# Sparse attention followed by a mixture of depths: half a mask, one count of ranks and one slot compare move between engines

## The chip, the core and the metric

The kernel runs on one core of one Trainium2 chip. The metric is the device time of one execution in microseconds. The median of three runs before the change is 803.54 us. Engines are named as in the profile: PE (TensorE, matmuls; PEld is its weight load), DVE (VectorE), ACT (ScalarE), POOL (GpSimd), SP (SyncE, which here only issues DMAs). Each engine works through its own instructions in order; semaphores order engines among each other.

## The reference

Attention keeps, for each query, only the 32 largest of its 576 scores. Its output is the input of a mixture of depths: the 128 tokens of each batch with the highest gate go through a two-layer network, the others are passed on as they are.

```python
B, H, S, D = 8, 8, 576, 64          # q, k, v: (8, 8, 576, 64) f32
scores = q @ k.T / sqrt(D)
kth = 32nd largest score of each row
attn = softmax(where(scores >= kth, scores, -1e9))
x = (attn @ v) as (B, S, H * D)     # (8, 576, 512)

gate = x @ w_gate                   # (8, 576)
for b in range(B):
    top = the 128 tokens with the largest gate[b]
    h = maximum(x[b, top] @ w1, 0)  # (128, 1024)
    y = h @ w2                      # (128, 512)
    out[b] = x[b]
    out[b, top] = x[b, top] + sigmoid(gate[b, top]) * y
```

## The kernel before

**Units and steps.** The 576 query rows of a batch are cut into five tiles: four of 128 rows, and one of 64 (t = J = 4). A unit is one tile and two heads (four heads for the last tile), so a batch has 4 * 4 + 2 = 18 units and the kernel N = 144. The main loop runs `for n in range(-1, N)`, and step n does something for several units at once, so that the engines overlap: the scores of unit n + 1 on TensorE and their copy `sc` on ScalarE, the bound search of unit n on VectorE, the comparison with the bound of unit n - 1 on ScalarE and GpSimd, the exact 32nd value of unit n - 2 on VectorE, the masks of unit n - 3, and the transposition, exponential and value matmul of unit n - 4. The text calls n modulo 18 the position of a step in its batch; position 0 of batch b is n = 18 b.

**The search on VectorE.** `find_bound` takes the eight largest of each of seven stretches of 82 or 83 scores (14 instructions `cand<-sc` for the two halves of a unit), then reduces these (`best`, `bound`) to the 24th largest of the candidates. ScalarE forms the sign of each score against that bound (`sides`, with the sum in `seen`, lines 561 to 568; `sign` is called once early in a step and once after the score copy). GpSimd multiplies scores and signs (`y`, line 1115) and adds a short filling (`fill`). VectorE takes the eight largest of `y` (`next`); the last of these is the 32nd score.

**The mask.** `mask` (line 585) writes 0 for scores that stay, and something positive for others, in `less`. The first half of a unit goes to ScalarE (Relu with a bias, line 594), the second to GpSimd (`tensor_scalar`, is_lt). In the steps of `scatter_steps` (line 1041: n = 54, 72, 90, 108, 126 and 137) GpSimd has a scatter of rows to issue, and the second half goes to VectorE instead: the pair of engines is `(act, None)`, and None stands for `compare`, an is_lt that also sums. It is put off to the middle of the step's bound search by `vector_late`. TensorE then turns the scores and adds the mask (`turn`, line 633), ScalarE takes the exponential (`pT`).

**The mixture.** When all tiles of a batch have been divided and their gates formed (`dot`, line 979), `mixture` (line 761) runs as a generator, piece by piece, in steps of the next two batches given by `mix_at`. For batches 0 to 6, in this order:

- position 5: `split` on GpSimd (the gates in three bf16 parts); two small DMAs write the gates to DRAM, a third reads them back to every partition as `gate_row`, 128x576.
- positions 7, 9, 10, 13, 14, one for each tile t: `choose` counts on VectorE how many gates are larger than each of the tile's own (`junk<-gate_row,gate`, sum in `ranks`); then a comparison of the rank with the slot numbers 0 to 127 gives `pick`, a 0/1 matrix. For t = 0 that comparison is on VectorE as well, for others on GpSimd (`choose_slot` through `pool_late`). What is put off runs in the step after, so the first tile's is at position 8. Batch 6 uses the closer list of line 1029; its first two tiles are both put off to n = 133.
- position 16: `multiply_places` multiplies `pick` with `parts` into a few free columns of PSUM, which gives each slot its token and gate; then the rows are fetched, multiplied with w1 and w2 at positions 1 to 17 of the batch after, and scattered back with addition (`add_rows`) at position 0 of the one after that.

**What is put off, and where it runs.** `late` is emptied by `flush` on ScalarE's and others' part of the step, before the score copy; `vector_late` between the two halves of the bound search; `pool_late` after the bound search and before GpSimd's products `y`.

```python
for b in rest:
    next(mixtures[b], None)
```

**The end.** After the loop the last units are finished without overlap of further ones, the last batch's mixture is done with its own code (lines 1350 to 1569), and a check is made: several reductions give `sure`, 1 for each partition if all shortcuts were exact; the sum of all ranks must also be that of 0 to 575 for each batch. If not, `tc.If(is_unsure > 0)` runs `general`, which does all eight batches over again in a slower, exact way.

Of the kernel before, what the change touches and what calls it, by code (L numbers as in the profile page):

```python
# [10 lines left out]
AF = mybir.ActivationFunctionType  # L11
ALU = mybir.AluOpType
FP32 = mybir.dt.float32
BF16 = mybir.dt.bfloat16
# [5 lines left out]
CAP = 128  # L20
# [28 lines left out]
def kernel(  # L49
# [11 lines left out]
    nc = tc.nc  # L61
    P = nc.NUM_PARTITIONS
    B, H, S, D = q.shape
# [3 lines left out]
    NT = J + 1  # L67
# [3 lines left out]
    DE = D + 1  # L71
    NDC = HD // P
    NFC = F // P
    scale = 1.0 / float(D) ** 0.5 / SMALLER
# [3 lines left out]
    const = ctx.enter_context(tc.tile_pool(name="const", bufs=1))  # L78
# [40 lines left out]
    for i in range(2):  # L119
        gate = const.tile([P, NT], FP32, name=f"gate{i}")  # L120
        nc.gpsimd.memset(gate, 0.0)
        parts = const.tile([P, NT, 2, 3], BF16, name=f"parts{i}")
        nc.gpsimd.memset(parts, 0.0)
        nc.vector.tensor_copy(out=parts[:, :, 0, 0:2], in_=parts_i)
        gates_of.append((gate, parts))
    slot_i = const.tile([P, CAP], I32, name="slot_i")
    nc.gpsimd.iota(slot_i, pattern=[[1, CAP]], base=0, channel_multiplier=0)
# [25 lines left out]

    ranks = const.tile([P, B, NT], FP32, name="ranks")
    nc.gpsimd.memset(ranks, 0.0)

    others = const.tile([P, NT], FP32, name="others")
    nc.gpsimd.memset(others, 0.0)
# [43 lines left out]

    late, vector_late, pool_late = [], [], []
# [180 lines left out]
    def bank(pool, name, **how):  # L384
        return pool.tile([P, 512], FP32, name=name, **how)
# [199 lines left out]
    def mask(sc, next8, on=None):  # L585

        less = wkpool.tile([P, 2, S], BF16, name="less")  # L590
        for i, engine in enumerate(on or (act, pool)):
            kth = next8[:, i, 7:8]
            if engine is act:
                act.activation(less[:, i, :], sc[:, i, :], AF.Relu, bias=kth, scale=-1.0)
            else:

                def is_less(engine=engine, i=i, kth=kth):
                    if engine is None:
                        compare(less[:, i, :], sc[:, i, :], kth, ALU.is_lt)
                        return  # L600
                    engine.tensor_scalar(
                        out=less[:, i, :],
                        in0=sc[:, i, :],
                        scalar1=kth,
                        scalar2=None,
                        op0=ALU.is_lt,
                    )

                if engine:
                    is_less()  # L610
                else:
                    vector_late.insert(0, is_less)
        return less

    def turn_some(tr, z, less):
# [142 lines left out]
            rank[0:n, t : t + 1], rank[0:n, t : t + 1], tok[0:n, 1:2], ALU.add  # L758
        )

    def mixture(row0, pg, rank, exact=False):

# [28 lines left out]


        pick = modpool.tile([P, NT, CAP], BF16, name="pick")
        for t in range(NT):
            yield
            n = R if t == J else P

            def choose(t=t, n=n):  # L800
                junk = modpool.tile([P, S], FP32, name="junk", tag="scratch")
                dve.tensor_scalar(
                    out=junk[0:n, :],
                    in0=gate_row[0:n, :],
                    scalar1=gate[0:n, t : t + 1],
                    scalar2=None,
                    op0=ALU.is_gt,
                    op1=ALU.add,
                    accum_out=rank[0:n, t : t + 1],
                )  # L810
                if exact:
                    break_ties(t, gate, gate_row, rank)

                if t == 0:
                    compare(pick[:, t, :], slot, rank[:, t : t + 1], ALU.is_equal)
                else:
                    pool_late.append(lambda: choose_slot(t, n))

            def choose_slot(t, n):
                pool.tensor_scalar(  # L820
                    out=pick[0:n, t, :],
                    in0=slot[0:n, :],
                    scalar1=rank[0:n, t : t + 1],
                    scalar2=None,
                    op0=ALU.is_equal,
                )

            vector_late.append(choose)

# [2 lines left out]
            ps = ps_misc.tile([P, 512], FP32, name="place_ps", tag="misc")  # L832
        else:
            ps = values_bank[0]
        ps = ps[:, 2 * DE : 2 * DE + 6]


        done = B if exact else int(row0) // S + 1
        row_i = modpool.tile([P, 1], I32, name="row_i", bufs=2)
        g = modpool.tile([P, 1], FP32, name="g", bufs=2)  # L840
        multiply_places(ps, pick, pg)
        found = stats.tile([P, 6], FP32, name="found", bufs=2)
        place = stats.tile([P, 2], FP32, name="place", bufs=2)
        kept.append(lambda ps=ps: act.copy(out=found, in_=ps))

# [62 lines left out]
    def multiply_places(ps, pick, pg):  # L908

        for t in range(NT):  # L910
            n = R if t == J else P
            pe.matmul(
                ps,
                pick[0:n, t, :],
                pg[1][0:n, t, :, :].rearrange("p a e -> p (a e)"),
                start=(t == 0),
                stop=(t == J),
            )

    def split(gate, parts):  # L920

        rest = modpool.tile([P, NT], FP32, name="rest")
        pool.tensor_copy(out=parts[:, :, 1, 0], in_=gate)
        pool.tensor_tensor(rest, gate, parts[:, :, 1, 0], ALU.subtract)
        pool.tensor_copy(out=parts[:, :, 1, 1], in_=rest)
        pool.tensor_tensor(rest, rest, parts[:, :, 1, 1], ALU.subtract)
        pool.tensor_copy(out=parts[:, :, 1, 2], in_=rest)

    def add_parts(place, found):
        dve.tensor_reduce(  # L930
            out=place,
            in_=found.rearrange("p (a e) -> p a e", e=3),
            axis=mybir.AxisListType.X,
            op=ALU.add,
        )
# [201 lines left out]
    def mask_of(n, on=None):  # L1137
        b, i = divmod(n, per_batch)
        masks[n] = mask(scs[n], next8s[b][:, i, :, :], on)
        if i == per_batch - 1 and b < B - 1:  # L1140
            keep_least(b, bounds.pop(b)[:, :, :, 7], next8s.pop(b)[:, :, :, 7])

    for n in range(-1, N):
# [60 lines left out]
        if is_unit(n - 4):  # L1204
            turn_rest()()
        if is_unit(n - 3):
            mask_of(n - 3, (act, None) if n in scatter_steps else None)
        flush()
        if is_unit(n + 1) and n + 1 >= NHP:
            b, i = divmod(n, per_batch)  # L1210
# [55 lines left out]
        if gating is not None:  # L1266
            b, t = gating
            if t == J:
                store(out[b], of_batch[b][0])
                mixtures[b] = mixture(float(b * S), of_batch[b][1], ranks[:, b, :])  # L1270
        for b in rest:
            next(mixtures[b], None)
        b, i = divmod(n, per_batch)
# [153 lines left out]
    for t in (J - 1, J):  # L1427
# [6 lines left out]
            op0=ALU.subtract,  # L1434
            op1=ALU.is_equal,
        )
    ps = bank(ps_end, "av3")[:, 0:6]
    place = stats.tile([P, 2], FP32, name="place", bufs=2)
    row_i = modpool.tile([P, 1], I32, name="row_i", bufs=2)
    g = modpool.tile([P, 1], FP32, name="g", bufs=2)  # L1440
# [2 lines left out]
    keep_rows(place, row_i, float((B - 1) * S), float(B * S - 1))  # L1443
    xe = modpool.tile([P, HD], FP32, name="xe")
    fetch_rows(xe, out, row_i)
    dve.tensor_scalar_max(out=g, in0=place[:, 1:2], scalar1=-88.0)
    act.activation(g, g, AF.Exp, scale=-1.0)
    for _ in between:
# [42 lines left out]
    for what, op, than, limit in (  # L1491
        (bounded, ALU.min, ALU.is_gt, LEAST),
        (least, ALU.min, ALU.is_gt, LEAST),
        (low, ALU.min, ALU.is_gt, 0.5),
        (seen, ALU.max, ALU.is_lt, float(MIDDLE)),
        (seen, ALU.min, ALU.is_gt, float(MIDDLE - 16)),
        (sums.rearrange("p t h -> p (t h)"), ALU.min, ALU.is_gt, FEWEST),
        (sums.rearrange("p t h -> p (t h)"), ALU.max, ALU.is_lt, MOST),
    ):
        far = stats.tile([P, 1], FP32, name="far", bufs=2)  # L1500
        dve.tensor_reduce(out=far, in_=what, axis=mybir.AxisListType.X, op=op)
        dve.scalar_tensor_tensor(
            out=sure, in0=far, scalar=limit, in1=sure, op0=than, op1=ALU.mult
        )

    far = stats.tile([P, 1], FP32, name="far", bufs=2)
    dve.tensor_reduce(out=far, in_=ranks, axis=mybir.AxisListType.XY, op=ALU.add)
    dve.tensor_tensor(sure, sure, far, ALU.add)
    far = stats.tile([P, 1], FP32, name="far", bufs=2)
    dve.tensor_reduce(out=far, in_=others, axis=mybir.AxisListType.X, op=ALU.add)  # L1510
    dve.tensor_tensor(sure, sure, far, ALU.add)
    ones = stats.tile([P, 1], FP32, name="ones", bufs=1)
    dve.memset(ones, 1.0)
    unsure = const.tile([1, 1], I32, name="unsure")
# [2 lines left out]
    for f0 in range(0, NFC, 2):  # L1517
# [20 lines left out]
        out=unsure,  # L1538
        in0=ps[0:1, 0:1],
        scalar1=-1.0,  # L1540
        scalar2=float(P + B * (S * (S - 1) // 2)),
        op0=ALU.mult,
        op1=ALU.add,
    )
# [133 lines left out]
```

## Time and profile before

| | us |
|---|---|
| median of 3 runs | 803.54 |
| runs | 805.48, 803.54, 802.9 |
| profiled execution, its own time | 802.83 |
| span of its instructions in the profile | 800.5 |
| VectorE busy in the span | 771.6 |
| ScalarE, TensorE, GpSimd busy | 728.4, 728.1, 706.4 |
| granted TensorE clock, mean | 0.997 |

The 2.3 us between the profiled execution and its span lie outside the instructions. Busy time is the union of an engine's recorded instructions. A recorded instruction on VectorE, ScalarE or GpSimd overlaps its successor a little (the 288 `next` instructions have a mean of 751 ns, while two of them in a row start 0.67 us apart), so what one costs is read from the starts. Nearly all of the kernel's calls pass through one helper, so they carry its line, L45, and are told apart by the tiles they write and read.

### The profile page before, as it was taken

How to read it: one execution, taken by the hardware profiler on the slowest of the kernel's cores; microseconds unless marked ns; L12 is line 12 of the kernel's file. 1: busy time of each engine (PE TensorE's matmuls, PEld its weight loads, DVE VectorE, ACT ScalarE, POOL GpSimd, SP SyncE). 2: the span in 40 equal slices, each digit the busy share in tenths (PEclk: the TensorE clock that was granted, in tenths of full speed). 3: DMA queues.
4: the chain of work that ended last, by engine and by line, in shares of the span. 5: the costliest groups of instructions: out<-in, count | busy, mean ns of one | idle time of the engine just before them, and what ended most of it. 6: DMA issues, size and time to landing. Idle time of an engine off the chain costs nothing. (4 is left out here: it accounts for less than half of the span.)

```text
span 800.5 us, 33285 instructions
## 1 busy us (share of the span) xinstructions
PE 728.1 (91%) x12535; PEld 550.2 (69%) x12535; DVE 771.6 (96%) x4655; ACT 728.4 (91%) x1577; POOL 706.4 (88%) x722
## 2 busy tenths in 40 slices
PE   8888888788999999999999989999899999999887
PEld 6766666656876668766786667866687667767756
DVE  7999999999999999999999999999999999999962
ACT  6999999999999999999999999999999999989830
POOL 4899999899999999999999999999999999999921
PEclk9999999999999999999999999999999999999999
DMA  8941114121241132221251221502234102101021
GB/s 170 293 95 43 42 62 103 29 54 29 70 107 42 29 94 63 64 55 41 69 109 29 56 41 62 113 20 54 42 90 89 29 8 75 24 6 25 3 74 31
DMA packets 121752, 50.70 MB, mean 63 GB/s; under 512 B 116016, under 2 KB 116016, under 8 KB 120560
## 3 DMA queue, kind: packets, MB, share of 16 engines
q1 hardware_dynamic: 118368, 43.94, 22.2%
q0 software_dynamic: 1744, 4.20, 2.8%
q8 instruction: 101, 1.65, 0.9%
q10 hardware_dynamic: 1472, 0.36, 0.2%
q14 instruction: 67, 0.55, 0.2%
HBM read 36.93 MB, written 11.55 MB: 61 GB/s over the span
## 5 line engine op out<-in xcount | busy, mean ns | idle before, releaser
L45 POOL TENSOR_TENSOR y<-sc,sides 128x576 f32<-128x576 f32 x288 | 366.9, 1304 | 17.7 <-ACT sides L45 16.6
L45 DVE MAX8 cand<-sc 128x8 f32<-128x82 f32 (+1 forms) x2016 | 314.4, 228 | 3.0 <-ACT sc L45 3.0
L45 POOL TENSOR_SCALAR less<-sc,next 128x576 bf16<-128x576 f32 x135 | 232.5, 1722 | 38.4 <-DVE next L45 34.2
L45 ACT ACTIVATE sides<-sc,bound 128x576 bf16<-128x576 f32 x288 | 229.6, 797 | 17.0 <-DVE bound L45 13.1
L45 PEld LDWEIGHTS av<-v,pT 128*64 128x64 f32 x4608 | 146.9, 138 | 91.4 <-ACT last L45 83.8
L45 DVE MAX8 next<-y 128x8 f32<-128x584 f32 x288 | 204.4, 751 | 0.0
L45 PE MATMUL av<-v,pT 128*64 128x65 f32 x4608 | 166.9, 225 | 38.9 <-ACT last L45 38.4
L45 PEld LDWEIGHTS <-less 64*128 64x128 bf16 (+1 forms) x2448 | 157.6, 129 | 29.3 <-POOL less L45 24.6
L45 PE MATMUL ps<-kT,qT 64*128 64x288 f32 (+1 forms) x1248 | 170.1, 422 | 0.3 <-ACT sc L45 0.3
L45 PE MATMUL ptr<-out_of_reach,less 64*128 64x64 bf16 x2272 | 151.0, 190 | 17.3 <-POOL less L45 16.6
L45 PE MATMUL ptr<-ident,sc 64*128 64x64 f32 x2272 | 166.3, 252 | 0.0
L45 ACT ACTIVATE pT<-ptr 128x1024 f32<-128x1024 f32 x142 | 147.7, 1040 | 14.5 <-PE ptr L45 12.7
L45 ACT COPY sc<-ps 128x1152 f32<-128x1152 f32 x140 | 159.6, 1140 | 0.0
L45 PEld LDWEIGHTS ptr<-ident,sc 64*128 64x128 f32 x2272 | 138.6, 137 | 23.8 <-issue 21.2
L45 ACT ACTIVATE less<-sc,next 128x576 bf16<-128x576 f32 x141 | 110.5, 784 | 0.0
L45 PEld LDWEIGHTS ps<-kT,qT 64*128 64x128 f32 (+1 forms) x1248 | 92.8, 176 | 17.6 <-ACT sc L45 0.4
L45 DVE MATCH_REPLACE8 cand<-best,cand 128x21 f32<-128x21 f32 (+1 forms) x576 | 98.8, 179 | 0.0
L45 DVE MAX8 best<-cand 128x8 f32<-128x21 f32 (+1 forms) x576 | 90.4, 189 | 0.0
L45 ACT ACTIVATION_READ_ACCUMULATOR sides<-sc,bound 128x1 f32 x288 | 62.0, 215 | 0.0
L45 PE MATMUL h_ps<-xeT,w 128*128 128x128 f32 x464 | 61.9, 278 | 0.0
L45 PEld LDWEIGHTS av<-ident,sc 128*128 128x128 f32 x144 | 20.0, 139 | 54.8 <-issue 44.9
L45 PE MATMUL av<-vpair,last 128*64 128x130 f32 x576 | 56.9, 276 | 0.0
(165 smaller groups left out, 925.2 us busy)
## 6 DMA issues: line engine op xcount, KB each, us to landing
v<-in_v_dram SPq DMA_DIRECT2D x64, 128.0 KB, 3.7
out_dram<-x SPq DMA_DIRECT2D x8, 1024.0 KB, 4.1
rows<-in_k_dram SPq DMA_DIRECT2D x56, 128.0 KB, 2.8
rows<-in_q_dram SPq DMA_DIRECT2D x56, 128.0 KB, 2.9
w<-in_moe_w_dram SPq DMA_DIRECT2D x2, 2048.0 KB, 10.3
gate_row<-row_dram SPq DMA_DIRECT2D x7, 288.0 KB, 4.6
last<-in_q_dram SPq DMA_DIRECT2D x8, 128.0 KB, 3.6
vpair<-in_v_dram SPq DMA_DIRECT2D x16, 64.0 KB, 4.8
```

The lines of the kernel that those rows point to most:

```text
L45: return lambda *a, **kw: self._tc.keep_in_program_order(fn(*a, **kw))
```

## The change

Four things are changed.

1. In `scatter_steps` both halves of the mask are on ScalarE, `(act, act)`; `mask` no longer has a VectorE form.
2. In the mixtures of batches 0 to 6 the first tile's count is made on ScalarE: the sum of Sign(gate - gate_row) over the 576 gates. With r gates larger than one's own that sum is 575 - 2 r. It is put off through `late`; the signs themselves are written over `pick` and not used.
3. The first tile's comparison with the slots goes to GpSimd, which compares the sum with `slot_signs` = 575 - 2 * slot.
4. `parts` has a seventh column of ones, so `multiply_places` also counts how many tokens each slot received. These counts are kept in `places` for all batches, and the check at the end asks that each be one, in place of the sum of the ranks.

```diff
@@ constants
-        parts = const.tile([P, NT, 2, 3], BF16, name=f"parts{i}")
+        parts = const.tile([P, NT, 7], BF16, name=f"parts{i}")
         nc.gpsimd.memset(parts, 0.0)
-        nc.vector.tensor_copy(out=parts[:, :, 0, 0:2], in_=parts_i)
+        nc.gpsimd.memset(parts[:, :, 6:7], 1.0)
+        nc.vector.tensor_copy(out=parts[:, :, 0:2], in_=parts_i)
...
+    signs = const.tile([P, B - 1], FP32, name="signs")
+    places = const.tile([P, B, 7], FP32, name="places")
+    nc.gpsimd.memset(places, 1.0)
+    slot_signs = const.tile([P, CAP], FP32, name="slot_signs")
+    nc.vector.tensor_scalar(
+        out=slot_signs, in0=slot, scalar1=-2.0, scalar2=float(S - 1),
+        op0=ALU.mult, op1=ALU.add,
+    )
@@ mixture
         for t in range(NT):
             yield
             n = R if t == J else P
+
+            def weigh_gates():
+                act.activation(
+                    pick.rearrange("p t c -> p (t c)")[:, 0:S],
+                    gate_row,
+                    AF.Sign,
+                    bias=gate[:, 0:1],
+                    scale=-1.0,
+                    accum_out=sign_sum,
+                )
+                pool_late.append(lambda: choose_slot(0, P, slot_signs, sign_sum))
+
+            if t == 0 and not exact:
+                late.append(weigh_gates)
+                continue
...
-                if t == 0:
-                    compare(pick[:, t, :], slot, rank[:, t : t + 1], ALU.is_equal)
-                else:
-                    pool_late.append(lambda: choose_slot(t, n))
+                pool_late.append(lambda: choose_slot(t, n))
...
-        ps = ps[:, 2 * DE : 2 * DE + 6]
+        ps = ps[:, 2 * DE : 2 * DE + 7]
...
-        found = stats.tile([P, 6], FP32, name="found", bufs=2)
+        found = places[:, 0 if exact else done - 1, :]
@@ main loop
-            mask_of(n - 3, (act, None) if n in scatter_steps else None)
+            mask_of(n - 3, (act, act) if n in scatter_steps else None)
@@ end
     fetch_rows(xe, out, row_i)
+    act.copy(out=places[:, B - 1, 6:7], in_=ps[:, 6:7])
...
+        (places[:, :, 6], ALU.min, ALU.is_gt, 0.5),
+        (places[:, :, 6], ALU.max, ALU.is_lt, 1.5),
...
-    dve.tensor_reduce(out=far, in_=ranks, axis=mybir.AxisListType.XY, op=ALU.add)
-    dve.tensor_tensor(sure, sure, far, ALU.add)
-    far = stats.tile([P, 1], FP32, name="far", bufs=2)
-    dve.tensor_reduce(out=far, in_=others, axis=mybir.AxisListType.X, op=ALU.add)
-    dve.tensor_tensor(sure, sure, far, ALU.add)
```

More of the change, by code (lines that the diff above doesn't have):

```diff
@@ L155 @@
     nc.gpsimd.memset(ranks, 0.0)
+    signs = const.tile([P, B - 1], FP32, name="signs")
[3 more added lines that the diff above has]
+    nc.vector.tensor_scalar(
+        out=slot_signs,
+        in0=slot,
+        scalar1=-2.0,
+        scalar2=float(S - 1),
+        op0=ALU.mult,
+        op1=ALU.add,
+    )
     others = const.tile([P, NT], FP32, name="others")
@@ L595, in mask @@
             else:
[L597 to L610, printed above, removed]
-                else:
-                    vector_late.insert(0, is_less)
+                engine.tensor_scalar(
+                    out=less[:, i, :],
+                    in0=sc[:, i, :],
+                    scalar1=kth,
+                    scalar2=None,
+                    op0=ALU.is_lt,
+                )
         return less
@@ L759, in break_ties, with mixture @@
         )
-    def mixture(row0, pg, rank, exact=False):
+    def mixture(row0, pg, rank, exact=False, sign_sum=None):
         gate = pg[0]
@@ L795, in mixture, with choose_slot @@
         pick = modpool.tile([P, NT, CAP], BF16, name="pick")
+        rank_of = rank
+        def choose_slot(t, n, slot=slot, rank=None):
+            if rank is None:
+                rank = rank_of[:, t : t + 1]
+            pool.tensor_scalar(
+                out=pick[0:n, t, :],
+                in0=slot[0:n, :],
+                scalar1=rank[0:n, :],
+                scalar2=None,
+                op0=ALU.is_equal,
+            )
         for t in range(NT):
@@ L798, in mixture @@
             n = R if t == J else P
+            def weigh_gates():
[6 more added lines that the diff above has]
+                    accum_out=sign_sum,
+                )
+                pool_late.append(lambda: choose_slot(0, P, slot_signs, sign_sum))
+            if t == 0 and not exact:
+                late.append(weigh_gates)
+                continue
             def choose(t=t, n=n):
@@ L812, in choose @@
                     break_ties(t, gate, gate_row, rank)
-                if t == 0:
-                    compare(pick[:, t, :], slot, rank[:, t : t + 1], ALU.is_equal)
-                else:
-                    pool_late.append(lambda: choose_slot(t, n))
[L819 to L826, printed above, removed]
+                pool_late.append(lambda: choose_slot(t, n))
             vector_late.append(choose)
@@ L914, in multiply_places @@
                 pick[0:n, t, :],
-                pg[1][0:n, t, :, :].rearrange("p a e -> p (a e)"),
+                pg[1][0:n, t, :],
                 start=(t == 0),
@@ L922, in split @@
         rest = modpool.tile([P, NT], FP32, name="rest")
[L923 to L927, printed above, removed]
+        pool.tensor_copy(out=parts[:, :, 3], in_=gate)
+        pool.tensor_tensor(rest, gate, parts[:, :, 3], ALU.subtract)
+        pool.tensor_copy(out=parts[:, :, 4], in_=rest)
+        pool.tensor_tensor(rest, rest, parts[:, :, 4], ALU.subtract)
+        pool.tensor_copy(out=parts[:, :, 5], in_=rest)
     def add_parts(place, found):
@@ L931, in add_parts @@
             out=place,
-            in_=found.rearrange("p (a e) -> p a e", e=3),
+            in_=found[:, 0:6].rearrange("p (a e) -> p a e", e=3),
             axis=mybir.AxisListType.X,
@@ L1269 @@
                 store(out[b], of_batch[b][0])
-                mixtures[b] = mixture(float(b * S), of_batch[b][1], ranks[:, b, :])
+                mixtures[b] = mixture(
+                    float(b * S),
+                    of_batch[b][1],
+                    ranks[:, b, :],
+                    sign_sum=signs[:, b : b + 1],
+                )
         for b in rest:
@@ L1436 @@
         )
-    ps = bank(ps_end, "av3")[:, 0:6]
+    ps = bank(ps_end, "av3")[:, 0:7]
     place = stats.tile([P, 2], FP32, name="place", bufs=2)
@@ L1504 @@
         )
-    far = stats.tile([P, 1], FP32, name="far", bufs=2)
-    dve.tensor_reduce(out=far, in_=ranks, axis=mybir.AxisListType.XY, op=ALU.add)
-    dve.tensor_tensor(sure, sure, far, ALU.add)
-    far = stats.tile([P, 1], FP32, name="far", bufs=2)
-    dve.tensor_reduce(out=far, in_=others, axis=mybir.AxisListType.X, op=ALU.add)
-    dve.tensor_tensor(sure, sure, far, ALU.add)
     ones = stats.tile([P, 1], FP32, name="ones", bufs=1)
@@ L1540 @@
         scalar1=-1.0,
-        scalar2=float(P + B * (S * (S - 1) // 2)),
+        scalar2=float(P),
         op0=ALU.mult,
```

## The prediction, made before the changed kernel was run

> **What bounds the kernel now.** I read the page's busy shares first, then the busy time of one batch's 18 steps, then the waits, then the instructions of two steps one by one.
>
> ```profile
> PE 728.1 (91%) x12535; PEld 550.2 (69%) x12535; DVE 771.6 (96%) x4655; ACT 728.4 (91%) x1577; POOL 706.4 (88%) x722
> ```
>
> Four engines are nearly full, so shares alone decide nothing. Batch 5's steps (its scores; n = 90 to 107), cut at position 9, in the columns PE, PEld, DVE, ACT, POOL:
>
> ```profile
> 471.75:518.31 46.56, 44.23 (x790) 36.00 (x786) 46.45 (x287) 45.60 (x101) 43.97 (x45) 1.00 0.34 82
> 518.31:566.33 48.02, 45.10 (x767) 30.91 (x767) 47.99 (x291) 45.31 (x98) 44.23 (x44) 1.00 0.17 41
> ```
>
> VectorE is idle for 0.14 of 94.58 us. The others have 3.7 us (ScalarE), 6.4 (GpSimd) and 5.3 (TensorE) to spare, mostly in the second half. The waits of that batch (engine waiting, for whom; us in total, times, longest):
>
> ```profile
> POOL less L45 <- DVE next L45: 5.5, 10, 1.0
> ...
> ACT sides L45 <- DVE bound L45: 2.2, 5, 0.6
> PE ptr L45 <- POOL less L45: 2.2, 7, 0.6
> ```
>
> GpSimd and ScalarE wait for VectorE; no line has VectorE waiting. So in the loop the time is the sum of VectorE's instructions. From the timeline (start, us), position 0 (n = 90, a scatter's step), and below it position 8 (n = 98):
>
> ```profile
> 472.77 0.79 DVE L45 TENSOR_SCALAR_CACHE_REDUCE less<-sc,next 128x576 bf16<-128x576 f32 x1
> 473.49 0.08 DVE L45 DVE_READ_ACCUMULATOR less<-sc,next 128x1 f32 x1
> 473.49 1.11 DVE L45 MAX8 cand<-sc 128x8 f32<-128x82 f32 x7
> ```
>
> ```profile
> 512.38 1.10 DVE L45 MAX8 cand<-sc 128x8 f32<-128x82 f32 x7
> 513.40 0.18 DVE L45 RECIPROCAL rden<-sums 128x8 f32<-128x8 f32 x1
> 513.50 0.76 DVE L45 TENSOR_SCALAR_CACHE_REDUCE junk<-gate_row,gate 128x576 f32<-128x576 f32 x1
> 514.19 0.08 DVE L45 DVE_READ_ACCUMULATOR junk<-gate_row,gate 128x1 f32 x1
> 514.31 0.34 DVE L45 TENSOR_SCALAR_CACHE_REDUCE pick<-slot,ranks 128x128 bf16<-128x128 f32 x1
> 514.58 0.08 DVE L45 DVE_READ_ACCUMULATOR pick<-slot,ranks 128x1 f32 x1
> 514.58 1.11 DVE L45 MAX8 cand<-sc 128x8 f32<-128x82 f32 x7
> ```
>
> An instruction starts before the last one's recorded end, so its price is the distance between starts, not its duration. The mask costs 473.49 - 472.77 = 0.72 us; the count with the first slot's compare costs 514.58 - 513.50 = 1.08, of which 0.12 is the compare's wait for the rank.
>
> **The change part by part.**
>
> *Removed from VectorE.* The mask goes from six steps (n = 54, 72, 90, 108, 126, 137): 6 x 0.72 = 4.3 us. Count and compare go from seven mixtures: six at 1.08, and the seventh (n = 133, where the next tile's count follows) 1.11 from 697.81 to 698.92: 7.6 us. Together 11.9. Whole steps say the same: position 0 without a mask (n = 36) lasts 4.74 against 5.47, position 8 5.93 against 4.80 for a step that also has a reciprocal (n = 102), so 6 x 0.73 + 7 x 1.13 = 12.3. I take 11.9.
>
> *Added to ScalarE.* A mask half and a Sign with a sum, priced by ScalarE's own rows:
>
> ```profile
> 475.93 0.78 ACT L45 ACTIVATE sides<-sc,bound 128x576 bf16<-128x576 f32 x1 [0.65 <-DVE bound L45]
> 476.62 0.19 ACT L45 ACTIVATION_READ_ACCUMULATOR sides<-sc,bound 128x1 f32 x1
> 476.71 0.26 ACT L45 ACTIVATE last<-av 128x128 f32<-128x128 f32 x1
> 476.87 0.76 ACT L45 ACTIVATE less<-sc,next 128x576 bf16<-128x576 f32 x1
> 477.53 0.63 ACT L45 COPY kT<-ps 128x256 f32<-128x256 f32 x2
> ```
>
> The mask is 477.53 - 476.87 = 0.66. The Sign with its accumulator read is 0.78 here, and 0.77 over the loop. A batch gains 1.43 us of ScalarE, all in positions 0 to 8. Both kinds already run there under the trace's single table load, so no load is added. TensorE's wait for VectorE's mask at a scatter (0.2 in this batch) goes; GpSimd's mask is then the last that it waits for, as elsewhere. Queued behind them are the copies of K and Q, the score copy of the next step, and the second Sign, for which GpSimd's products wait.
>
> Is there room? Positions 0 to 8: VectorE falls to 46.56 - 1.80 = 44.76, ScalarE rises to 45.60 + 1.43 = 47.03. It falls back by at most 2.3 us. Positions 9 to 17: 48.02 against 45.31, so 2.7 us are made up before the next batch. VectorE does not feel this while its inputs are early, and they are. At n = 98 it starts on scores at 512.38 and on products at 516.98. These were ready at 509.63 and 513.18:
>
> ```profile
> 508.38 1.25 ACT L45 COPY sc<-ps 128x1152 f32<-128x1152 f32 x1
> ```
>
> ```profile
> 512.97 0.21 POOL L45 TENSOR_TENSOR y<-steps,seen 128x16 f32<-128x16 f32 x1
> ```
>
> That is 2.75 us ahead with ScalarE already about 0.95 late there (its first Sign of a step starts 0.95 after the bound that it needs), 3.8 when it is on time. A lateness of 2.3 leaves 1.5. So the cost is nothing; what hides it is VectorE's own stock of finished scores.
>
> The skill's page "ScalarE: Activation LUTs" (Rules for kernel authors) speaks against this move: simple elementwise work belongs on VectorE, up to about 3 times as fast in bf16. By that rule a 576-wide pass would cost VectorE some 0.24 us (0.72 / 3, an estimate from page and row), 13 passes 3.1, and with 7 x 0.39 for compares and bubbles the gain would be 5.9 us, the time 797.6. The rows say 0.72: with an f32 source and a sum, VectorE takes as long as ScalarE. I follow the rows.
>
> *Added to GpSimd.* Seven compares of 128x128. Three in a row run from 706.35 to 708.08, 0.577 each: 4.0 us. Each stands at position 8 behind the division and ahead of the two products. It waits for the Sign, which ScalarE issues before the second Sign that the products wait for anyway, so it adds work and no new wait. The products of n = 97 end 0.58 later than at 518.54, at 519.1. VectorE reads them 1.08 earlier than about 522.3 (518.31, plus 3.4 as in step 98 without its 1.08 and the reciprocal, plus 0.6 for a dot), at 521.2: 2.1 us are left. The next mask half follows later, and TensorE's turn waits for it (0.6 once per batch now, perhaps 1.5 then); that again makes ScalarE late, not VectorE. GpSimd's positions 0 to 8 hold 43.97 + 0.58 = 44.6 us of work in 44.76.
>
> *Data.* The Sign needs gate_row. In batch 5 its load is issued at 501.8 and takes 4.6 us, while the Sign would start at about 513.7; for the seventh mixture it is issued at 690.4 and needed at about 697.9, still 2.9 us to spare. No transfer is moved.
>
> *Start and end.* One more VectorE instruction (slot_signs) at 3.8 us: the nearest row, 128x128, took 0.23; VectorE then idles until 4.85. Three more memsets on GpSimd, whose last one ended at 4.18, 0.03 to 0.1 each: 0 to 0.2 us, and TensorE's first transpose at 4.37 stood behind its own warm-up; I take 0. At the end four small reductions and products are replaced by four (0.6 us either way), done 2.5 us before TensorE needs their result at 788.11. The extra ScalarE copy of one column (about 0.2) fits into the 0.85 that ScalarE idles before Exp at 776.23. Seven columns instead of six in a 0.17 us matmul: nothing.
>
> Sum: -11.9 us. The profiled execution took 802.83 (span 800.5), so 790.9; on the median of 803.54, 791.6.
>
> **The rivals.**
>
> *VectorE begins to wait.* GpSimd's later mask holds up TensorE, that ScalarE, that the scores, and the 2.1 us melt at positions 8 to 10. For it: GpSimd fills 44.6 of 44.76 us, and TensorE, ScalarE and GpSimd wait for each other in a ring. Against it: every observed lateness is made up within three steps. If half of six times 1.08 and a third of six times 0.72 is given back (6 x 0.54 + 6 x 0.24 = 4.7): 796.3.
>
> *ScalarE becomes the bound.* Its batch is 90.9 + 1.43 = 92.3 against VectorE's 92.8. If its waits of about 1.5 us (pT, and Signs) cannot be removed, a batch takes 93.8, only 0.8 less than now: 6 x 0.8, about 799. Against it: most of these waits exist because it is ahead.
>
> *Slower: the end's check fails.* Exactness decides. At its own place a gate gives Sign(0), which must add exactly 0; if it added 1 or -1, the sum would have the wrong parity for every slot, slots of the first tile stay empty, and the new check (0.5 < filled < 1.5) sends all eight batches through the general path. That path needs 14 passes of 576 per unit on VectorE; two of 584 take 1.33 (470.42 to 471.75), so 144 x 14 x 0.67 = 1,350 us at least: over 2,100. One unfilled slot is enough. Nothing in this trace shows a Sign of exact zero, so the case stays open. It is also the case in which the change does not do what it says.
>
> **How the numbers follow.** VectorE stays the bound: 0.77, giving 791.6 (790.3 to 793). It waits in part: 0.13, 793 to 798. ScalarE the bound: 0.06, 798 to 802. Check fails: 0.04. A measurement here tells about 0.3% (2.4 us) from no change, so half of the ScalarE case counts as the same: faster 0.93, same 0.03, slower 0.04. Downwards the range takes 12.3 for 11.9, the lowest of the three runs and some of the tail's waits: 789.5. Upwards it takes most of the second case: 796.
>
> **What would show it.** Right: steps at positions 0 and 8 of about 4.75 and 4.85 us; VectorE still 99.8% busy between 100 and 740; ScalarE's and GpSimd's busy time up by 9.4 and 4.0; scores still 1 us or more ahead of VectorE. Wrong: idle time of VectorE before cand (waiting for sc) or next (waiting for y), above all at positions 8 to 10; the general path's instructions after the last scatter.

## The result, and the profile after

| | before | changed |
|---|---|---|
| median, us (runs) | 804.27 (4) | 793.24 (4) |
| range, us | 802.90 to 805.48 | 792.51 to 794.72 |
| profiled execution / its span, us | 802.83 / 800.5 | 794.72 / 792.5 |
| VectorE, ScalarE, GpSimd busy, us | 771.6, 728.4, 706.4 | 763.2, 732.9, 713.5 |

The ratio is 0.9866, with a 95% interval of 0.9842 to 0.9889. In a later set of runs the changed kernel took 794.18 (793.98 to 795.72) beside 802.93 (14 runs, 802.38 to 805.28): 0.9895, 0.988 to 0.991. So the change brings 8.7 to 11.0 us; the profiled pair (a long run of the changed kernel, a short one of the kernel before) differs by 8.0 of span.

The page's busy line of the changed kernel:

```profile
PE 726.9 (92%) x12535; PEld 551.2 (70%) x12535; DVE 763.2 (96%) x4616; ACT 732.9 (92%) x1598; POOL 713.5 (90%) x732
```

Batch 5 again, from the start of n = 90 to that of n = 99 and on to n = 108 (columns PE, PEld, DVE, ACT, POOL):

```profile
467.56:512.26 44.70, 42.77 (x778) 34.77 (x774) 44.63 (x281) 44.53 (x100) 42.85 (x45) 1.00 0.35 86
512.26:560.67 48.41, 46.22 (x781) 32.14 (x779) 48.38 (x290) 46.98 (x102) 46.42 (x45) 1.00 0.17 41
```

The first half lasts 44.70 in place of 46.56: the 1.86 that mask and count were worth. But the second half lasts 48.41 in place of 48.02, though nothing was added to VectorE there. VectorE is still idle for 0.10 of 93.11 us. The waits of this batch that answer to those shown of before have shrunk, since GpSimd and ScalarE have less slack behind VectorE (one other has grown: GpSimd's products wait for ScalarE's Sign, 0.2 us before and 1.2 now):

```profile
POOL less L45 <- DVE next L45: 1.8, 4, 0.5
...
PE ptr L45 <- POOL less L45: 1.0, 3, 0.4
...
ACT sides L45 <- DVE bound L45: 0.4, 1, 0.4
```

VectorE's timeline, first at position 0 (14 stretches without a mask between them), then at position 8 (no count, no compare, only the reciprocal):

```profile
467.56 2.12 DVE L45 MAX8 cand<-sc 128x8 f32<-128x82 f32 x14
```

```profile
507.46 1.10 DVE L45 MAX8 cand<-sc 128x8 f32<-128x82 f32 x7
508.48 0.18 DVE L45 RECIPROCAL rden<-sums 128x8 f32<-128x8 f32 x1
508.58 1.07 DVE L45 MAX8 cand<-sc 128x8 f32<-128x82 f32 x7
```

What went to ScalarE at position 8 stands back to back there (start, us):

```profile
508.51 0.77 ACT L45 ACTIVATE less<-sc,next 128x576 bf16<-128x576 f32 x1
509.18 0.76 ACT L45 ACTIVATE pick<-gate_row,gate 128x576 bf16<-128x576 f32 x1
509.84 0.19 ACT L45 ACTIVATION_READ_ACCUMULATOR pick<-gate_row,gate 128x1 f32 x1
509.93 0.36 ACT L45 COPY kT<-ps 128x256 f32<-128x256 f32 x1
```

The Sign and its accumulator cost 509.93 - 509.18 = 0.75, forecast 0.77.

**Where the second half's 0.4 us lies.** At position 9 the only VectorE instruction that changed is the gate's dot, which was neither moved nor edited. VectorE and GpSimd around it, first before the change:

```profile
519.62 0.67 DVE L45 CUSTOM_DVE_ANT_0 prod<-x,wg 128x512 f32<-128x512 f32 x1
520.22 0.08 DVE L45 DVE_READ_ACCUMULATOR2_ANT gate<- 128x1 f32 x1
```

```profile
515.85 2.51 POOL L45 TENSOR_TENSOR y<-sc,sides 128x576 f32<-128x576 f32 x2
518.33 0.21 POOL L45 TENSOR_TENSOR y<-steps,seen 128x16 f32<-128x16 f32 x1
518.59 1.72 POOL L45 TENSOR_SCALAR less<-sc,next 128x576 bf16<-128x576 f32 x1
```

and after it:

```profile
513.57 1.07 DVE L45 CUSTOM_DVE_ANT_0 prod<-x,wg 128x512 f32<-128x512 f32 x1
514.58 0.08 DVE L45 DVE_READ_ACCUMULATOR2_ANT gate<- 128x1 f32 x1
```

```profile
510.95 0.61 POOL L45 TENSOR_SCALAR pick<-slot_signs,signs 128x128 bf16<-128x128 f32 x1
511.53 2.52 POOL L45 TENSOR_TENSOR y<-sc,sides 128x576 f32<-128x576 f32 x2
514.00 0.72 POOL L45 TENSOR_TENSOR y<-steps,seen 128x16 f32<-128x16 f32 x1
```

Before, the dot started 1.26 us after the end of GpSimd's products (518.36) and cost 520.22 - 519.62 = 0.60. Now it starts 0.48 us ahead of their end (511.53 + 2.52 = 514.05) and costs 514.58 - 513.57 = 1.01. Its end lies 0.58 behind the start of GpSimd's next instruction (514.58 - 514.00), so it needs about its usual 0.60 once the products are over; in turn that next instruction, GpSimd's small filling, which took 0.21, takes 0.72 and ends as the dot ends. All of this is recorded as busy time, on both engines. No wait row shows it, and that is why VectorE looks as full as before. The view of the tile `prod` (duration of its 40 dots in ns: least, median, most) before and after:

```profile
L45 DVE CUSTOM_DVE_ANT_0 prod<-x,wg x40: 668/680/1596, 50.3 to 771.0; 128x512 f32<-128x512 f32 x32, 64x512 f32<-64x512 f32 x8
```

```profile
L45 DVE CUSTOM_DVE_ANT_0 prod<-x,wg x40: 672/818/1596, 50.5 to 763.0; 128x512 f32<-128x512 f32 x32, 64x512 f32<-64x512 f32 x8
```

The Trainium skill describes such a meeting ("SBUF — State Buffer", section "Who interferes with whom"): a VectorE instruction with two inputs in SBUF needs a port that GpSimd reads through, whoever starts first keeps it for its whole instruction, and the other stands still. No run here shows that it is this port; the rows show only which engine stands still, and when. Against GpSimd's products they agree, to about 0.1 us (0.48 + 0.60 = 1.08, measured 1.01). Against GpSimd's `less`, with one input, they do not: a dot that starts 0.46 us after `less` loses 0.15 us and not the 1.26 that are left of it. Two such rows of before, at position 5:

```profile
498.72 0.82 DVE L45 CUSTOM_DVE_ANT_0 prod<-x,wg 64x512 f32<-64x512 f32 x1
```

```profile
498.26 1.72 POOL L45 TENSOR_SCALAR less<-sc,next 128x576 bf16<-128x576 f32 x1
```

A start of 0.63 us or more into `less` costs nothing (0.74, 0.78 and 1.03 in this trace, 0.63 at position 3 of the changed kernel). For `less` the measurement decides: only about its first 0.62 us exclude the dot.

### The profile page after: what moved, and what is told of

Its sections match the earlier page's. It is cut to its first block, busy times and chain, and to the rows that moved or that the text cites. A ratio compares the mean times of both kernels' runs of the same rounds, so it can differ in the third digit from the quotient of the medians.

```text
span 792.5 us, 33266 instructions
## 1 busy us (share of the span) xinstructions
PE 726.9 (92%) x12535; PEld 551.2 (70%) x12535; DVE 763.2 (96%) x4616; ACT 732.9 (92%) x1598; POOL 713.5 (90%) x732
## 5 line engine op out<-in xcount | busy, mean ns | idle before, releaser
L45 PEld LDWEIGHTS <-less 64*128 64x128 bf16 (+1 forms) x2448 | 160.2, 131 | 20.3 <-POOL less L45 15.9
L45 PE MATMUL ptr<-ident,sc 64*128 64x64 f32 x2272 | 164.2, 253 | 0.0
L45 ACT ACTIVATE less<-sc,next 128x576 bf16<-128x576 f32 x147 | 115.2, 787 | 0.0
```

The source lines that it names most:

```text
L45: return lambda *a, **kw: self._tc.keep_in_program_order(fn(*a, **kw))
```

## The experiments

The theory: VectorE's own instructions set the loop's time; what the change saved is all there, and part of it is given back by dots that now meet GpSimd's products. The rivals: the lateness of ScalarE costs time; the end of the kernel gave it back.

**One part at a time: the mask, the count.** `mask_only` leaves the count, the compare and the check as before and moves only the masks; `count_only` keeps the old masks:

```diff
 mask_only (against before)
-            mask_of(n - 3, (act, None) if n in scatter_steps else None)
+            mask_of(n - 3, (act, act) if n in scatter_steps else None)
 count_only (against the changed kernel)
 ...   (the mask's VectorE form, put back)
-            mask_of(n - 3, (act, act) if n in scatter_steps else None)
+            mask_of(n - 3, (act, None) if n in scatter_steps else None)
```

> The kernel before with only the mask half of the six scatter steps moved to ScalarE. Theory (VectorE's sum decides, and a gain is given back only where its dot meets GpSimd's products): position 0 falls from 5.47 to 4.74 us, the dot of position 9 stays at 0.60, so 6 x 0.73 = 4.4 us less than before, about 799.5. Rival (ScalarE and GpSimd are full and give back part of what VectorE gains): clearly less than 4.4 us, with idle time of VectorE before cand or next.

Measured: 799.03 us (798.04 to 801.24), 0.995 (0.9934 to 0.9966). The masks' steps last 4.74 in place of 5.47, and the dots of position 9 stay at 0.60. In four of the six batches position 8 became longer by 0.09 (5.93 to 6.02), and so did n = 133, which was not forecast. In batch 5 the time lies ahead of the first slot's compare, which starts 0.21 behind the read of the rank in place of 0.12. Batch 2 had this already in the kernel before (6.02 at n = 44); why it spread stays open.

> The changed kernel with the mask half of the scatter steps back on VectorE, so only the first tile's count and slot compare are moved. Theory: position 8 falls by 1.12, but the dot of position 9 rises from 0.60 to 1.00 us because it now meets GpSimd's products; 6 x (1.12 - 0.40) + 1.1 - 0.4 = about 5.0 us less than before, near 799. Rival (the dots grew because of the mask's move or of a general lateness): dots at 0.60 and 7.9 us less, near 796.

Measured: 799.85 us (796.04 to 801.11), 0.9946 (0.9925 to 0.9967). The six executions lie 5 us apart, so the trace says more: its loop is 4.99 shorter than before (table below), forecast about 5.0. Position 8 falls by 1.12 and position 9 grows by 0.40, as in the changed kernel. So it is the count's move that brings the dot and the products together: VectorE comes 1.12 earlier to position 9 and GpSimd's products 0.58 later, and 1.26 - 1.12 - 0.58 = -0.44 (-0.48 in the trace of the changed kernel). With the mask left where it was, ScalarE is early again (1.37 us of scores in stock at position 9, against 0.95), and yet the 0.40 is there. That speaks against the rival of a late ScalarE.

**The dot at another place.** The dot is asked for inside the bound search, ahead of the third stretch of the second half. Here it waits for four stretches more, 4 x 0.146 us:

```diff
-                if (i, u) == (1, 2) and amid_late:
+                if (i, u) == (1, 6) and amid_late:
```

> The changed kernel with the gate's dot four MAX8 (0.58 us) later in the step (after the sixth stretch of the second half, not the second). Nothing else is changed. Theory: a dot that no longer meets GpSimd's two-input products or the first 0.6 us of its mask takes 0.60 everywhere: six dots of position 9 fall by 0.40, some twelve of positions 5 and 13 by 0.15, the two at n = 135 and 139 by 0.38 and 0.58: 5 us less than the changed kernel, about 788. Rival (the dot's place does not matter; what is lost against the forecast is lost to late inputs): no difference from the changed kernel, 793.

Measured: 788.05 us (786.9 to 788.58), 0.9807 (0.9792 to 0.9823). Its dots, and position 9 of batch 5 on VectorE and on GpSimd:

```profile
L45 DVE CUSTOM_DVE_ANT_0 prod<-x,wg x40: 662/674/1016, 51.4 to 756.2; 128x512 f32<-128x512 f32 x32, 64x512 f32<-64x512 f32 x8
```

```profile
510.82 0.69 DVE L45 CUSTOM_DVE_ANT_0 prod<-x,wg 128x512 f32<-128x512 f32 x1
511.44 0.08 DVE L45 DVE_READ_ACCUMULATOR2_ANT gate<- 128x1 f32 x1
```

```profile
509.47 1.28 POOL L45 TENSOR_TENSOR y<-sc,sides 128x576 f32<-128x576 f32 x1
510.70 0.22 POOL L45 TENSOR_TENSOR y<-steps,seen 128x16 f32<-128x16 f32 x1
510.90 2.20 POOL L45 TENSOR_SCALAR less<-sc,next 128x576 bf16<-128x576 f32 x1
```

The dot now starts 0.08 ahead of `less`. It takes 511.44 - 510.82 = 0.62, and `less` pays: 2.20 in place of 1.72. GpSimd can afford that here, VectorE could not. The loop becomes 6.0 us shorter than the changed kernel's (table below), beside the 8.9 that the change itself brought there.

> The kernel before, with the gate's dot asked for four units of work later (at (1, 6) in place of (1, 2)); nothing else is changed. Theory (the dot is lengthened by whatever GpSimd operation it meets): in the trace of before, 17 of the 38 dots start 0.46 us or less after GpSimd's less and pay 0.15 each, and the first two pay 0.93 and 0.33, in all 3.8 us above 0.60; with the dot away from those starts up to that much comes back, so 799 to 801, about -3 against before, if the new place meets no GpSimd operation of its own. Rival (the place of the dot is worth 5 us only to the changed kernel, because it alone has a full GpSimd): 0, 803.

The same line in the kernel before: 800.18 us (799.73 to 802.49), 0.997 (0.9959 to 0.9981). The gain is 2.75 us. The kernel before already paid for such meetings, at positions 5 and 13 and in its first batch.

**The account.** The starts of n = 2 and n = 142 in each trace give the loop's length; the dots' prices (from start to start) are summed over the 37 that lie between.

| kernel | loop, us | its dots, us | the rest |
|---|---|---|---|
| before | 731.10 | 25.68 | 705.42 |
| before, dot later | 728.39 | 22.93 | 705.46 |
| mask alone | 727.47 | 25.98 | 701.49 |
| count alone | 726.11 | 28.62 | 697.49 |
| changed | 722.17 | 29.11 | 693.06 |
| changed, again | 721.94 | 28.84 | 693.10 |
| changed, dot later | 716.14 | 23.10 | 693.04 |
| the same, again | 716.43 | 23.30 | 693.13 |

Without dots the changed loop is shorter by 705.42 - 693.06 = 12.36 us, and it is 693.1 wherever the dots are put. The dots give back 29.11 - 25.68 = 3.43. At 0.60 each they would cost 22.2. The two parts alone, 3.93 and 7.93, fall 0.5 short of the 12.36: most of it is the five times 0.09 of `mask_only`, which go where the compare has left VectorE.

**ScalarE's margin.** A useless Sign with a sum (0.77 us) is added ahead of the real one in each of the seven mixtures: to the changed kernel (`extra_sign`), then to the one with the later dot, once and twice (`dot_late_sign1`, `dot_late_sign2`):

```diff
 ...   (a tile spare for its sum)
             def weigh_gates():
+                for e in range(1):     # range(2) in dot_late_sign2
+                    act.activation(
+                        pick.rearrange("p t c -> p (t c)")[:, 0:S],
+                        gate_row,
+                        AF.Sign,
+                        bias=gate[:, 0:1],
+                        scale=-1.0,
+                        accum_out=spare[:, e : e + 1],
+                    )
                 act.activation(
```

> The changed kernel with a second, useless Sign over the gates ahead of the real one, into the same scratch and a sum of its own: 0.77 us more on ScalarE at position 8 in seven mixtures. Theory (VectorE is the bound and has scores 0.95 us in stock at position 9 at the lowest): no wait of VectorE, the time stays within 0.5 us of the changed kernel. Rival (ScalarE is the bound by now): 7 x 0.77 = 5.4 us more, near 798.6.

Measured: 795.53 us (795.27 to 795.79), 0.9902 (0.9885 to 0.9919). The median lies between the two forecasts, 1.35 above the 794.18 of the changed kernel's own later set, but the intervals of the two ratios overlap (0.988 to 0.991 there), so only the traces can tell. Without the dots the loop is 692.98 us, as before the Sign; VectorE does not wait, though only 0.04 to 0.08 us of its scores' stock is left. The dots are up by 0.86 to 29.97, because GpSimd waited for the later Sign and its products ended later. Batch 5's dot, and GpSimd beside it:

```profile
516.16 1.31 DVE L45 CUSTOM_DVE_ANT_0 prod<-x,wg 128x512 f32<-128x512 f32 x1
```

```profile
515.64 1.29 POOL L45 TENSOR_TENSOR y<-sc,sides 128x576 f32<-128x576 f32 x1 [0.16 <-ACT sides L45]
516.89 0.66 POOL L45 TENSOR_TENSOR y<-steps,seen 128x16 f32<-128x16 f32 x1
```

So a late ScalarE did reach VectorE, by way of the dot and not by way of the scores. Beside the loop, its profiled run starts 1.9 us later than the changed kernel's (17.43 against 15.49 at n = 2) and ends 2.1 sooner; both go with TensorE's clock (see the part on the end of the kernel).

> The changed kernel with the dot four units later once more, as the base of the two beside it: 787 to 789.

> The changed kernel with the later dot, and one useless Sign with a sum (0.77 us) per mixture on ScalarE, so that the cost of a late ScalarE is seen without the dot's meetings with GpSimd. At position 9 the scores lie 0.76 to 0.83 us ahead of VectorE in the trace with the later dot alone, and one Sign took 0.9 of such a stock in the changed kernel. Theory (a late ScalarE costs nothing until the stock is gone, and the 0.8 us that the Sign cost the changed kernel came from the dot): VectorE waits 0.1 us at most per batch, so +0 to +0.7 us against the run beside it. Rival (the Sign's own lateness costs time, by a way that no wait shows): +1 or more, with all dots still at 0.60.

> The same with two useless Signs per mixture. Theory (the stock of 0.8 us is the whole margin): the second Sign is paid in full by VectorE, 0.77 to 0.9 us in each of six batches, as a wait for ACT's sc at position 9: +4.5 to +6 us against the run with the later dot alone. Rival (the three units of products ahead, or the slack of the other steps, take it up as well): +2 or less.

Measured, in one set: 787.96 (786.49 to 789.4), 789.55 (789.46 to 789.56) and 797.39 (795.97 to 798.69). One Sign costs 1.6 us between the medians, more than the first theory's 0.7 and with the dots nearly at 0.60 (23.68 in all): its forecast was missed. The loop is 1.1 longer in the profiled runs: the step ahead of position 9 grew by 0.10 to 0.13 us in four batches and by 0.28 in one, where VectorE now runs out of scores, and 0.4 is in the dots. The two profiled executions differ by 2.8 us in all; 0.5 of that is the start and 1.2 the end, where only the one with the Sign lost TensorE's clock. For the second Sign the waits of VectorE in the loop say it plainly (one Sign above, two below):

```profile
DVE cand L45 <- ACT sc L45: 0.2, 1, 0.2
```

```profile
DVE cand L45 <- ACT sc L45: 6.4, 7, 1.5
```

The second Sign costs 7.8 us between the medians, not the 4.5 to 6 of the forecast. The wait alternates between 1.0 and 1.55 us from batch to batch: after a long one the stock of scores at position 8 is back at 1.99 us, after a short one only at 1.44, so part of the lateness is carried into the next batch. The trace has a likely carrier: TensorE stands idle for 2.06 us ahead of position 9 in five batches. In the three with the shorter waits it is then granted half its clock for 3.41 us (from 233.69, 421.42 and 609.15 us), in the other two it is not. Whether that makes the difference of 0.55 was not tested. The margin of the kernel with the later dot is therefore about one Sign per batch, and beyond it each microsecond on ScalarE costs more than one (7.8 us for 7 x 0.77 = 5.4). The changed kernel, whose dots hold VectorE back, has a little more of it (a stock of 0.95 us at position 9, against 0.8 and, in batch 2, 0.6).

**The end of the kernel.** In the profiled run of the changed kernel TensorE waits once for the last masks:

```profile
PE tr L45 <- DVE less L45: 2.2, 1, 2.2
```

and is then granted half its clock, for 6.8 us: in the first two rows below (columns as above; the clock is third from the end) (0.21 + 0.47) x 5 / 0.5. They are two stretches of the changed kernel, and behind them are the same with 30 useless matmuls in front of that wait:

```diff
     keep_gates(0, J - 1, rows_ps)
+    idle = bank(ps_misc, "idle", tag="misc")
+    for _ in range(30):
+        pe.matmul(idle[:, 0:P], out_of_reach, out_of_reach)
     mask_both(N - 3)
     weigh_unit(N - 3)
```

```profile
745.00:750.00 5.00, 2.77 (x57) 2.37 (x53) 5.00 (x24) 3.11 (x8) 4.47 (x6) 0.79 0.00 0
750.00:755.00 5.00, 5.00 (x82) 4.15 (x78) 5.00 (x11) 1.46 (x3) 0.90 (x2) 0.53 0.01 3
```

```profile
745.00:750.00 5.00, 5.00 (x106) 4.35 (x101) 5.00 (x22) 3.81 (x11) 4.49 (x5) 1.00 0.02 3
750.00:755.00 5.00, 5.00 (x134) 4.25 (x134) 4.97 (x13) 2.99 (x7) 0.55 (x2) 1.00 0.02 3
```

The value matmuls of unit N - 3 in the two:

```profile
750.99 2.00 PE L45 MATMUL av<-v,pT 128*64 128x65 f32 x32
```

```profile
750.00 1.15 PE L45 MATMUL av<-v,pT 128*64 128x65 f32 x32
```

> The changed kernel itself once more, so that the next two stand beside it in one set of runs: 792 to 795, the dots of position 9 again at about 1.00 us, twelve per cent of nothing else moved; start (first scores of VectorE) may differ by up to 2 us with the first DMA's landing.

> The changed kernel with 30 useless bf16 matmuls of 128x128 on TensorE ahead of the transposes of unit N - 3, into a PSUM bank that nothing else uses then, so that TensorE works through the 2.2 us in which it waits for VectorE's less at 746 us. Theory (the granted TensorE clock of 0.50 for the 6 us behind that wait lengthens the matmuls of units N - 3 and N - 2, and with them the tail): the clock stays at 1.0 there, the matmuls of unit N - 3 take 1.15 in place of 2.00 us, VectorE's last waits shrink, and the time falls by 1 to 2 us against the changed kernel in this set. Rival (the tail is set by VectorE, which has its own work there, and the late matmuls are hidden): within 0.4 us of the changed kernel though the clock is restored.

> The changed kernel with both: the dot four units later, and the 30 matmuls in the tail. If the two are independent: 788 less the gain of the matmuls alone, so 786 to 787; if the dot's new place had already shortened VectorE's part of the tail, no less than 787.7.

Measured, in one set: 794.18 (793.98 to 795.72), 792.64 (792.29 to 794.58) and 787.15 us (786.88 to 788.77; 0.9801, 0.9788 to 0.9813). The clock is restored, and from n = 142 to the end it takes 52.99 us in place of 54.21 in the changed kernel's profiled run of this set (1.2 less; the medians differ by 1.5, their ranges overlap). But the drop isn't there in every execution. The kernel with the later dot has a wait of 1.7 us with a drop in one profiled run (end 53.79 us), and one of 1.6 us without a drop in the other (52.76 us). Over all 13 profiled runs the end goes with the drop: 52.7 to 53.0 us in the five without one (the two with the matmuls among them), 53.8 to 54.2 in the six with 3.41 us of half clock, and 54.8 to 55.1 in the two with 6.83. By these ends the matmuls are worth 1 to 2 us in the executions that would have the drop, and nothing in others. Together with the later dot the median is 0.8 to 0.9 below the two medians of that kernel (788.05, 787.96), with ranges that overlap: the gain of both over the later dot alone is not settled. It is the lowest median measured, 16 us below before.

The start goes with the clock too. In three of the 13 (`count_only`, `extra_sign` and `dot_late_tail_busy`) n = 2 begins at 17.4 to 17.6 us, and TensorE's full clock is first recorded at 9.7 to 10.4; in the other ten it begins at 15.3 to 15.9, and the full clock stands at 3.8 to 6.1. The landing of the first load, which the expectation named, does not tell them apart: `after_again` and `extra_sign` begin the first copy of the keys at 5.17 and 5.18 us, and the first scores' matmuls behind it then take 0.48 us in the one and 0.81 in the other.

## Why the prediction was right, and where not

- **VectorE bounds the loop, and the time is the sum of its instructions.** Right. The loop without its dots fell by 12.36 us; the prediction's two sums were 11.9 and, from whole steps, 12.3. Of its two the whole steps were the better. Distances between the moved instructions leave out what they do to the next: the seven stretches behind the compare took 1.03 us before (514.58 to 515.61) and take 0.98 without it (508.58 to 509.56). Position 0 fell to 4.74 (forecast 4.75), position 8 to 4.81 (4.85), n = 133 by 1.13.
- **A constant dot.** This is the term that was mis-sized. The prediction put the dot into the second half as "0.6 for a dot". It cost 1.00 at position 9 in six batches, and with n = 135 and n = 139, where it met the start of a `less` (0.97 and 1.18), it gave back 3.4 us, over a quarter of the gain. One of the two numbers stood in the prediction's own sum: the products of n = 97, with their filling, were to end "at 519.1". The other stood in the trace of before: the dot of position 9, at 519.62, was to come 1.08 earlier, at 518.54. They had not been laid side by side. The trace of before showed what that means: a recorded 0.82 at position 5 for the dot that stands behind the start of a `less`, and 1.60 in the first batch for one that starts 1.05 ahead of the end of the products.
- **ScalarE's lateness costs nothing.** Right for the scores, and closer than the prediction had it. Behind the first batch its lateness peaked at 2.0 us (forecast at most 2.3). The stock of scores fell to 0.95 (forecast 1.5, and "still 1 us or more"): at position 9, not at position 8, whose 2.75 the estimate had started from. One more Sign used it up.
- **GpSimd's compare fits.** Right as to VectorE's waits: it takes 0.58 from start to start, and the products are 1.96 us early for VectorE at position 9 (forecast 2.1). But it moved those products under the dot.
- **Busy times "up by 9.4 and 4.0".** Missed: ScalarE's rose by 4.5, GpSimd's by 7.1. The new instructions on ScalarE are all there (6 and 7). But busy time is a union of recorded lengths, and an instruction with another right behind it is counted shorter: `pT` loses 3.5 us of it, though nothing about it has changed. On GpSimd the recorded fillings are 2.4 us longer in sum (34.7 to 37.1), beside the 4.3 of the compares; those behind the dots of position 9 went from 0.21 to 0.72.
- **The start and the end at nothing.** Within what the runs tell. In the profiled pair the loop begins 0.2 later and the end is 0.7 longer (54.84 against 54.12), so -8.9 + 0.2 + 0.7 = -8.0. The 0.7 goes with the clock: the run of before has 3.41 us of half clock there, the changed kernel's 6.83. Among the profiled runs of all these kernels the loop's start varies by 2.35 us and the end by up to 2.3, while the changed kernel's loop repeats within 0.3. Scatter of this size would account for one comparison giving 11.0 and the other 8.7; the executions without a profile do not show it.
- **The rule that speaks against the move** would have given 797.6, with VectorE's passes at a third of their price. Moving 6 masks took 0.73 us each off VectorE, so the rows were right and the rule did not apply to this f32 pass with a sum.
- **The rivals.** VectorE's wait for its inputs did not come, nor did ScalarE become the bound: VectorE has no wait between 60 and 735 us. The failing check did not come either: nothing of the general path runs after the last scatter, so Sign of an exact zero adds nothing to the sum. That the forecast of 791.6 lies within 1.7 us of the first median is partly luck: -12.4 and +3.4 make -8.9 in the loop, and the first comparison has 2 more than the loop lost.

## What to carry to other kernels

When an engine is the bound and never idle, a change of phase can still cost time inside its busy instructions: lay the new start of each two-input instruction beside what the neighbour engine will be doing then, and compare its recorded duration with its shortest one. Look for the row whose duration spreads (here 668 to 1,596 ns for the same shape); moving that instruction by half a microsecond may be worth as much as taking work away. And measure a margin at the position where it is thinnest, since a stock of 2.75 us at one step was 0.95 at the next.

## What the runs showed that was not expected

- A dot of 128x512 with both inputs in SBUF takes 0.60 us alone, 1.00 when it starts 0.48 ahead of the end of GpSimd's two-input products, and 1.24 at 0.77 ahead. When it starts first, GpSimd's instruction is the longer one (0.21 to 0.72 for the filling, 1.72 to 2.20 for `less`).
- GpSimd's one-input `less` of 1.72 us excludes the dot only in about its first 0.62 us.
- An idle time of TensorE of 1.3 to 2.2 us at the end was followed in eight of the eleven traces without the useless matmuls by 3.41 or 6.83 us at half the clock, worth 1 to 2 us, and in three by none. Its length does not decide: 1.35 us had the drop, 1.58, 1.94 and 2.22 had none, and of the five of 2.06 us in `dot_late_sign2` three had it. The Trainium skill ("TensorE: Matmul & The Clock Gate", What's actually happening) gives an idle window of about 3.4 us for that; these idle times are shorter.
- The new constant, a 128x128 `tensor_scalar` at the start, is recorded at 1.23 us on VectorE, where the estimate from the nearest row was 0.23. But the cast in front of it is recorded at 1.24, and was at 1.17 before the change, and the two end only 0.07 apart: nearly all of the 1.2 us was there already. Nothing waited for it.

```profile
2.71 1.24 DVE L153 CAST steps<-steps_i 128x16 f32<-128x16 int32 x1
2.79 1.23 DVE L164 TENSOR_SCALAR slot_signs<-slot 128x128 f32<-128x128 f32 x1
```
